# Transposing attention weights on VectorE and moving the blocks by DMA, in place of TensorE's transposes

## The chip, the cores and the metric

The kernel runs on one core of a Trainium2 chip. The metric is the time of one execution on the device in microseconds (us); several runs are taken and their median is given. The profile is that of one further execution. Its engines are TensorE (PE for matrix products, PEld for its loads of weights), VectorE (DVE), ScalarE (ACT), GpSimd (POOL) and SyncE (SP), which issues the DMA transfers here.

## The reference, cut to what matters

Four batches of attention with eight heads, 768 tokens and 64 features per head, followed by a gated feed-forward layer. Attention is local and blockwise at once: each token sees the tokens less than 16 away and, beside them, 24 summaries of blocks of 32 tokens (the maximum of the keys, the mean of the values).

```
k_sum = k.reshape(B, H, nb, block, D).max(axis=3)
v_sum = v.reshape(B, H, nb, block, D).mean(axis=3)
scores_l = where(|i - j| < 16, scale * q @ k.T, -1e9)
scores_s = scale * q @ k_sum.T + log(block)
a = softmax(concat(scores_l, scores_s))
x = a @ concat(v, v_sum)
...
xk = mu_k * x + (1 - mu_k) * x_prev ; xr = mu_r * x + (1 - mu_r) * x_prev
k = relu(xk @ w_k) ; out = sigmoid(xr @ w_r) * ((k * k) @ w_v)
```

## The kernel before

The work is cut into 32 units and 8 halves. A unit is one batch, one pair of heads and one half of the sequence (384 tokens, six windows of 64 queries); `unit` (L437) writes it down. A window sees 96 nearby keys and 24 block summaries, 120 columns in all (NK). A half is one batch and 384 tokens of the feed-forward layer: three gate products (`gate_tile`, L555) and eight expert steps (`experts`, L585), each a first product (L601) and a second product (L628).

In a unit, PE forms the scores of both heads into two PSUM tiles `sc` (L458). DVE applies the mask and takes the row's extreme (L469), ACT takes the exponential and its sum (L473), DVE inverts the sums (L479 and L480) and POOL scales the rows (L485). The weights then stand in the tiles `y` with queries on the partitions. The product with the values needs the keys on the partitions, so PE transposes three 128x120 blocks per head into a PSUM tile `pt` (L492), ACT copies them to SBUF as `pts` (L496), and PE multiplies by the values (L505). The result is copied into `vx` (L516 or L518), from which ACT, POOL and DVE make the inputs of the feed-forward layer (L527, L530, L533, L542, L544).

The transposes, the copies and the values product, cut from `unit`:

```
for i in range(NSL):
    nc.tensor.transpose(out=pt[h].t[0:NK, i * P:(i + 1) * P], in_=y[h].t[:, i, :], identity=ident_sb)
...
op("ACT", "pts", None, lambda h=h: nc.scalar.copy(
    out=pts[h].t, in_=pt[h].t[0:NK, 0:NSL * P].rearrange("p (i c) -> p i c", c=P)),
```

Loads of keys, values and queries (L359, L363, L441) go through SP. From batch 1 on the block means of the values come from a feature-major copy, loaded at L408, summed on DVE (L409), transposed on PE (L412), scaled on ACT (L429), and then spread by SP into six windows of each value tile (L432), SBUF to SBUF, two transfers per pair of heads. The feed-forward weights are loaded as words into the three staging tiles `st` (L323) and put together by ACT and DVE (L324, L327, L329); `split` (L333) makes a high and a low part of each, so that a full-precision product is three products of reduced-precision parts. In the first half of all, the first PLAIN expert steps (three here) skip the splitting and run as one plain fp32 product instead.

The order of all instructions is written out ahead by a planner (`Plan.schedule`, L143). Each operation has a cost from a table (LENGTH), the tiles it reads and writes, and a due time; each engine takes the operation that can start first, and among those ready the one that is due first. Operations inherit their due times from what follows them. The plan fixes the order of each engine's queue, SP's included; at run time semaphores decide when a step starts, and an engine never changes the order. The gate of half n is due at GATE1 + PERIOD x (n - 1), the first at GATE0; the units of a batch are due before its gate, UNITS apart from one another; the scores of a unit are due 10 us before the unit. SP takes a transfer at the earliest 20 us (EARLY) before it is due, keeps at most eight in flight (LANES) and costs 450 ns per issue (ISSUE) in the plan. Tiles come from pools of fixed size, most of them in the order in which the program asks for them: four `y`, three `pts` (one per head), three `st`, one `pt`, two `sc`, twelve `vx`.

Of the kernel before, what the change touches and what calls it, by code (L numbers as in the profile page):

```python
# [9 lines left out]
F32 = mybir.dt.float32  # L10
F32R = mybir.dt.float32r
U32 = mybir.dt.uint32
# [8 lines left out]
P = 128  # L21
NPAIR = H // 2
NS = S // BLOCK
QW = 64
# [17 lines left out]
    warm=223, kred=865, kred2=470, kmax=90, kcopy=280, vred=865, mask=204, rc=320, evac=470, mixd=535, sub=475, khv=280,  # L42
    result=600, wbits=340, wor=610, wsub=605, tiny=60,
    exp=380, pts=375, vm=160, mixa=515, cast=405, relu=380, square=425, sigmoid=500, sigmoid3=1600, wscale=570, wcast=530,
    norm=345, wcast_p=640, mixa_p=600, kcopy_p=450, evac_a=375,
)
TAIL = dict(PE=0, DVE=85, ACT=95, POOL=0, SP=0)
LATENCY = dict(PE=260, DVE=110, ACT=110, POOL=150, SP=0)
# [1 line left out]
DMA_FIXED = 2000  # L50
GATE0 = 34000
FULL = 34000
STEP0 = 4000
PLAIN = 3, 3
GATE1 = 76000
PERIOD = 50000
STEP = 4600
SLACK = 400
WARM = 260
WARM_END = 110000  # L60
GAP = 300
COLD = 5000
EARLY = 20000
ISSUE = 450
LANES = 8
TABLE = 1300
TABLES = dict(sigmoid=1, sigmoid3=1, exp=0, wscale=0)
LOCKS = {"wbits", "wor", "wsub", "mixd", "sub", "kcopy", "khv", "spread"}
FIRST = 4000
SECOND = 58000, 64000, 70000, 76000  # L70
UNITS = 5500


class Slot:
# [31 lines left out]
class Plan:  # L106
# [36 lines left out]
    def schedule(self):  # L143
# [29 lines left out]
        while any(ready.values()):  # L173
            best = None
            for e, now in engines.items():
                pick = fill = None
                if e == "PE" and now > WARM_END:
                    ready[e] = [x for x in ready[e] if x[0].name != "warm"]
                for o, at in ready[e]:
                    if o.name == "wcast" and len(free_slots["w"]) < owed + 2:  # L180
                        continue
                    if o.name == "warm":
                        fill = max(now, at), o
                        continue
                    start, need, ok = max(at, now, o.due - EARLY if e == "SP" else 0), {}, True
                    if e == "SP":
                        start = max(start, lanes[-LANES])
                    for x in o.bufs:
                        if x.place is None:
                            k = need.get(x.pool, 0)  # L190
                            if x.n not in (None, turn[x.pool] + k) or len(free_slots[x.pool]) <= k:
                                ok = False
                                break
                            start = max(start, free_slots[x.pool][k][0])
                            need[x.pool] = k + 1
                    if not ok:
                        continue
                    if any(max(start, engines[f]) + c < start + o.ways[e][0] for f, (c, _) in o.ways.items() if f != e):
                        continue
                    if e == "POOL" and o.name != "tiny" or e == "DVE" and o.name in LOCKS:  # L200
                        start = max(start, port)
                    late = start > now
                    load = e == "ACT" and TABLES.get(o.name, table) != table
                    key = (start if late else now, o.due + TABLE * load, o.n)
                    if pick is None or key < pick[0]:
                        pick = key, o, start
                if fill and (pick is None or pick[2] > fill[0] + GAP):
                    pick = None, fill[1], fill[0]
                if pick and (best is None or pick[2] < best[2]):
                    best = pick + (e,)  # L210
            assert best, "no operation can go on"
            _, o, start, e = best
            o.eng = e
            o.cost, o.emit = o.ways[e]
            owed += dict(wor=-1, wcast=1, wsub=-1).get(o.name, 0)
            for f in o.ways:
                ready[f] = [x for x in ready[f] if x[0] is not o]
            for x in o.bufs:
                if x.place is None:
                    _, x.place = free_slots[x.pool].pop(0)  # L220
                    turn[x.pool] += x.n is not None
            if e == "PE" and start < COLD:
                o.cost *= 1.6
            if e == "ACT" and TABLES.get(o.name, table) != table:
                o.cost += TABLE
                table = 1 - table
            o.start = start
            if e == "SP":
                engines[e] = start + ISSUE
                dma = max(dma, start + 600) + o.size * DMA_NS_PER_BYTE  # L230
                o.finish = dma + DMA_FIXED - 600
                lanes.append(o.finish)
            else:
                engines[e] = start + o.cost
                if e == "POOL" and o.name != "tiny" or e == "DVE" and o.name in LOCKS:
                    port = start + o.cost
                o.finish = start + o.cost + TAIL[e]
            for x in o.bufs:
                x.left -= 1
                if not x.left:  # L240
                    end = max(u.finish + LATENCY[u.eng] for u in x.users)
                    pool, places = self.later.get(x.pool, (x.pool, [x.place]))
                    free_slots[pool].extend((end, place) for place in places)
                    free_slots[pool].sort(key=lambda s: s[0])
            order.append(o)
            for s in o.succ:
                waiting[s] -= 1
                if not waiting[s]:
                    released(s)
# [4 lines left out]
def tile_kernel(ctx: ExitStack, tc: tile.TileContext, q, k, vT, v, mask, ident, pool, sel, mu, w_k, w_v, w_r, out):  # L254
# [7 lines left out]
    def slots(name, n, shape):  # L262
# [5 lines left out]
        ktx=[last_kt], w=slots("w", 2 * (NCK + 2 * NCV), [P, 512]),  # L268
        kt=tiles("kt", 3, [P, KL]), qt=tiles("qt", 4, [P, HT]), vx=tiles("vx", 12, [P, S + 1]),
        kg=tiles("kg", 2, [P, 49]), ks=tiles("ks", 2, [P, NS]),  # L270
        vs=tiles("vs", 1, [P, NS]), vm=tiles("vm", 4, [P, P]), sp=tiles("sp", 2, [P, P]),
        y=tiles("y", 4, [P, NSL, NK]), mn=tiles("mn", 4, [P, NSL]), sm=tiles("sm", 3, [P, 2 * NSL]),
        rc=tiles("rc", 3, [P, 2 * NSL]), pts=tiles("pts", 3, [NK, NSL, P]),
        z=tiles("z", 4, [P, DM]), xa=tiles("xa", 4, [P, HT]),
        xs=slots("xs", 16, [P, HT]), r=tiles("r", 2, [P, HT]),
        kh=tiles("kh", 2, [P, HT], F32R), kl=tiles("kl", 2, [P, HT], F32R),
# [76 lines left out]
    def load_set(b, p):  # L353
# [74 lines left out]
        else:  # L428
            op("ACT", "vm", None, lambda: nc.scalar.activation(  # L429
                vm.t[0:NS], tp.t[0:NS, 0:P], AF.Copy, scale=1.0 / BLOCK), reads=[(tp, 0)], writes=[(vm, 0)])  # L430
            for x in vw:
                op("SP", "load", None, lambda x=x: nc.sync.dma_start(  # L432
                    out=windows(x)[QW:KB], in_=vm.t[0:NS].unsqueeze(1).broadcast_to([NS, HW, P])),
                   reads=[(vm, 0)], writes=[(x, "b")], size=NS * HW * 512)
        return e

    def unit(b, p, hf, e, due):  # L437
# [6 lines left out]
        y = [buf("y") for _ in range(2)]  # L444
        mn = [buf("mn") for _ in range(2)]
        sm, rc = buf("sm"), buf("rc")
        pt = [buf("pt") for _ in range(2)]
        pts = [buf("pts") for _ in range(2)]
        av = buf("av")


        def scores():
# [7 lines left out]
                            start=True, stop=True,  # L460
                        )

        op("PE", "score", due - 10000, scores, reads=[*e["kparts"], (kt, "s"), (qt, 0)],
           writes=[(sc[0], 0), (sc[1], 0)])
        for h in range(2):
            for i in range(NSL):
                slot = hf * NSL + i
                var = 0 if slot == 0 else (2 if slot == 2 * NSL - 1 else 1)
                op("DVE", "mask", None, lambda h=h, i=i, var=var: nc.vector.tensor_tensor_reduce(  # L469
                    out=y[h].t[:, i, :], in0=sc[h].t[:, i, 0:NK], in1=mask_sb[:, var, :], scale=-SCALE, scalar=3.0e38,  # L470
                    op0=ALU.add, op1=ALU.min, accum_out=mn[h].t[:, i:i + 1]),
                   reads=[(sc[h], 0), *MASK], writes=[(y[h], i), (mn[h], i)])
                op("ACT", "exp", None, lambda h=h, i=i: nc.scalar.activation(  # L473
                    y[h].t[:, i, :], y[h].t[:, i, :], AF.Exp, bias=mn[h].t[:, i:i + 1], scale=-1.0,
                    accum_out=sm.t[:, NSL * h + i:NSL * h + i + 1]),
                   reads=[(y[h], i), (mn[h], i)], writes=[(y[h], i), (sm, NSL * h + i)])

# [5 lines left out]
        for h in range(2):  # L483
            for i in range(NSL):
                op("POOL", "norm", None, lambda h=h, i=i: nc.gpsimd.tensor_scalar(  # L485
                    out=y[h].t[:, i, :], in0=y[h].t[:, i, :], scalar1=rc.t[:, NSL * h + i:NSL * h + i + 1],
                    scalar2=1.0, op0=ALU.mult, op1=ALU.mult),
                   reads=[(y[h], i), (rc, 0)], writes=[(y[h], i)])

            def transposes(h=h):  # L490
                for i in range(NSL):
                    nc.tensor.transpose(out=pt[h].t[0:NK, i * P:(i + 1) * P], in_=y[h].t[:, i, :], identity=ident_sb)  # L492

            op("PE", "transpose", due - 3500 + 800 * h, transposes,
               reads=[(y[h], i) for i in range(NSL)] + [*IDENT], writes=[(pt[h], 0)])
            op("ACT", "pts", None, lambda h=h: nc.scalar.copy(  # L496
                out=pts[h].t, in_=pt[h].t[0:NK, 0:NSL * P].rearrange("p (i c) -> p i c", c=P)),
               reads=[(pt[h], 0)], writes=[(pts[h], 0)])

        def values():  # L500
            for w in range(HW):
                i, c = divmod(w, 2)
                for h in range(2):
                    hs = slice(h * D, (h + 1) * D)
                    nc.tensor.matmul(  # L505
                        av.t[hs, w * QW:(w + 1) * QW], windows(vw)[:, w, hs], pts[h].t[:, i, c * QW:(c + 1) * QW],
                        start=True, stop=True,
                    )

        op("PE", "values", due - 1000, values, reads=[(vw, x) for x in "ab"] + [(pts[0], 0), (pts[1], 0)],  # L510
           writes=[(av, 0)])
        if hf == 0:
            xt = xts[b, p] = buf("vx")
# [163 lines left out]
        weight("wv", j, w_v[j], j == NCV - 1)  # L677

    op("POOL", "tiny", -1.0e6, lambda: nc.gpsimd.memset(zero_sb, 0.0), writes=ZERO)
    spare = pools["pt"][0][:, 512 - P:512]  # L680
    for _ in range(WARM):
        op("PE", "warm", 1.0e8, lambda: nc.tensor.matmul(spare, zero_sb, zero_sb, start=True, stop=True), reads=ZERO)
# [123 lines left out]
```

## Time and profile before

| what | value |
|---|---|
| median of 3 runs | 449.93 us (449.85 to 450.32) |
| the profiled execution's own time | 450.6 us |
| its span, from the first to the last instruction | 448.8 us |
| granted clock of TensorE, mean over the span | 1.00 |
| transposes of the attention weights (L492) | 192 instructions |
| values products (L505) | 768 instructions, 24 a unit |
| transfers that spread the block means (L432) | 24 |

A line of the stretches view gives the busy time of each engine between two points of the span. A line of the chain gives when a piece began, how long it lasted and whose it was; the chain is followed back from the last instruction, at each step to what released it. An engine listed with q, as SPq or PEldq, is that engine's own queue of instructions. The profiled execution's own time is 1.8 us above its span, and 0.7 us above the median.

### The profile page before, as it was taken

To read this page: it belongs to the slowest core of one execution; us is meant where nothing else is said; L and a number is where in the kernel's file an instruction comes from. 1 tells how busy PE (TensorE), PEld (TensorE's weight loads), DVE (VectorE), ACT (ScalarE), POOL (GpSimd) and SP (SyncE) were. 2 spreads that over 40 slices of the span, in tenths; PEclk is the share of its full clock that TensorE was granted. 3 is DMA by queue.
4 is the path that set the end of the run, shared out by engine and by line. 5 is a ranking of instruction groups with operands and counts; after the bars stand their busy time and mean duration, and the time that the engine had idled before them with its cause. 6 is when DMAs were issued, how large, how long until landed. Compare 5 with 4: busy or idle time off the path is not lost.

```text
span 448.8 us, 9629 instructions
## 1 busy us (share of the span) xinstructions
PE 441.7 (98%) x3521; PEld 366.3 (82%) x3521; DVE 261.2 (58%) x866; ACT 282.9 (63%) x808; POOL 104.8 (23%) x237
## 2 busy tenths in 40 slices
PE   8999999999999999999999999999999999999996
PEld 8755578778888888978888888987888888888895
DVE  3889998995645763194655756175663455232213
ACT  3798999997765583288866655268966555232221
POOL 0561545561540012032432012002442001000000
PEclk9999999999999999999999999999999999999999
DMA  8967886831024275051007076031000010001001
GB/s 288 395 225 253 318 300 225 273 136 39 15 71 150 77 246 200 2 169 31 15 2 272 2 243 229 0 125 64 15 15 15 1 71 1 1 0 72 0 0 72
DMA packets 24230, 51.96 MB, mean 116 GB/s; under 512 B 2935, under 2 KB 10743, under 8 KB 24183
## 3 DMA queue, kind: packets, MB, share of 16 engines
q1 hardware_dynamic: 24183, 51.35, 33.3%
q8 instruction: 28, 0.46, 0.4%
q14 instruction: 19, 0.16, 0.1%
HBM read 43.28 MB, written 6.29 MB: 110 GB/s over the span
## 4 chain that ended last, share of the span: by engine, by line
PE 90%; ACT 3%; DMA 3%; DVE 2%; SPq 1%; issue 0%; DVEq 0%
PE mm L628 30%; PE mm L601 29%; PE av L505 5%; PE pt L492 5%; PE sc L458 4%; PE mm L562 4%; PE mm L564 4%; PE mm L563 4%; DMA vx<-in_v 3%; PE mm L575 2%; ACT y L473 1%; PE pt L412 0%; DVE z L658 0%; ACT pts L496 0%; PE mm L397 0%
## 5 line engine op out<-in xcount | busy, mean ns | idle before, releaser
L601 PE MATMUL mm<-xs,w 128*128 128x384 f32 x756 | 147.4, 343 | 0.0
L601 PEld LDWEIGHTS mm<-xs,w 128*128 128x128 f32 x756 | 132.9, 188 | 7.4 <-issue 0.7
L485 POOL TENSOR_SCALAR y<-y,rc 128x120 f32<-128x120 f32 x192 | 83.9, 455 | 142.1 <-DVE rc L480 117.1
L628 PE MATMUL mm<-w,kh 128*128 128x512 f32 x366 | 100.3, 402 | 0.2 <-ACT kh L615 0.2
L608 ACT ACTIVATE r<-mm 128x384 f32<-128x384 f32 x64 | 31.3, 489 | 95.7 <-PE mm L601 95.7
L473 ACT ACTIVATE y<-y,mn 128x120 f32<-128x120 f32 x192 | 73.7, 387 | 13.2 <-DVE mn L469 13.1
L628 PEld LDWEIGHTS mm<-w,kh 128*128 128x128 f32 x366 | 66.1, 188 | 12.6 <-ACT kh L615 0.5
L614 DVE CAST kh<-r 128x384 fp32r<-128x384 f32 x55 | 21.1, 384 | 92.6 <-ACT r L610 83.6
L628 PE MATMUL mm<-w,kl 128*128 128x512 f32 x183 | 57.0, 406 | 0.0
L469 DVE CUSTOM_DVE_ANT_0 y<-sc,mask_sb 128x120 f32<-128x120 f32 x192 | 42.5, 276 | 16.1 <-PE sc L458 16.0
L544 DVE TENSOR_TENSOR xs<-xa,xs 128x384 fp32r<-128x384 f32 x56 | 30.5, 551 | 32.8 <-ACT xs L542 32.6
L628 PEld LDWEIGHTS mm<-w,kl 128*128 128x128 f32 x183 | 32.9, 188 | 7.4 <-issue 0.5
L533 DVE SCALAR_TENSOR_TENSOR xa<-vx,mu_sb,xa 128x384 f32<-128x384 f32 x56 | 33.5, 627 | 8.2 <-POOL xa L530 4.2
L616 DVE TENSOR_TENSOR kl<-r,kh 128x384 fp32r<-128x384 f32 x61 | 34.7, 569 | 4.2 <-ACT kh L615 0.7
L473 ACT ACTIVATION_READ_ACCUMULATOR y<-y,mn 128x1 f32 x192 | 36.4, 189 | 0.0
L610 ACT ACTIVATE r<-r 128x384 f32<-128x384 f32 x64 | 33.7, 526 | 1.2
L505 PEld LDWEIGHTS av<-pts,vx 120*64 120x64 f32 x768 | 25.1, 137 | 10.2 <-issue 6.4
L562 PE MATMUL mm<-w,xs 128*128 128x512 f32 x84 | 33.3, 397 | 0.0
L492 PE MATMUL pt<-ident_sb,y 128*120 128x128 f32 x192 | 32.5, 278 | 0.8 <-ACT pts L496 0.6
L496 ACT COPY pts<-pt 120x384 f32<-120x384 f32 x64 | 30.1, 470 | 5.0 <-PE pt L492 4.3
L564 PE MATMUL mm<-w,xs 128*128 128x512 f32 x84 | 32.9, 392 | 0.0
L563 PE MATMUL mm<-w,xs 128*128 128x512 f32 x84 | 32.8, 390 | 0.0
(65 smaller groups left out, 505.1 us busy)
## 6 DMA issues: line engine op xcount, KB each, us to landing
vx<-in_v SPq DMA_DIRECT2D x32, 384.0 KB
kt<-in_k SPq DMA_DIRECT2D x15, 544.0 KB
qt<-in_q SPq DMA_DIRECT2D x32, 192.0 KB
out<-z SPq DMA_DIRECT2D x24, 256.0 KB
st<-in_vT SPq DMA_DIRECT2D x12, 384.0 KB
st<-in_w_k SPq DMA_DIRECT2D x8, 512.0 KB
st<-in_w_v SPq DMA_DIRECT2D x8, 512.0 KB
st<-in_w_r SPq DMA_DIRECT2D x4, 512.0 KB
```

The costliest lines, as they stand in the source:

```text
L469: op("DVE", "mask", None, lambda h=h, i=i, var=var: nc.vector.tensor_tensor_reduce(out=y[h].t[:, i, :], in0=sc[h].t[:, i, 0:NK], in1=mask_ ...
L473: op("ACT", "exp", None, lambda h=h, i=i: nc.scalar.activation(y[h].t[:, i, :], y[h].t[:, i, :], AF.Exp, bias=mn[h].t[:, i:i + 1], scale=-1.0,
L485: op("POOL", "norm", None, lambda h=h, i=i: nc.gpsimd.tensor_scalar(out=y[h].t[:, i, :], in0=y[h].t[:, i, :], scalar1=rc.t[:, NSL * h + i: ...
L492: nc.tensor.transpose(out=pt[h].t[0:NK, i * P:(i + 1) * P], in_=y[h].t[:, i, :], identity=ident_sb)
L505: nc.tensor.matmul(av.t[hs, w * QW:(w + 1) * QW], windows(vw)[:, w, hs], pts[h].t[:, i, c * QW:(c + 1) * QW], start=True, stop=True,)
L562: nc.tensor.matmul(ps.t, xh.t[:, ts], h, start=(p == 0), stop=False)
L563: nc.tensor.matmul(ps.t, xh.t[:, ts], l, start=False, stop=False)
L564: nc.tensor.matmul(ps.t, xl.t[:, ts], h, start=False, stop=(p == NPAIR - 1))
L601: nc.tensor.matmul(ps.t[:, 0:HT], w.t[:, p * P:(p + 1) * P], x[p][s].t, start=(n == 0), stop=(n == len(terms) * NPAIR - 1))
L610: op("ACT", "square", None, lambda: nc.scalar.activation(r.t, r.t, AF.Square), reads=[(r, 0)], writes=[(r, 0)])
L616: op("DVE", "sub", None, lambda: nc.vector.tensor_tensor(out=kl.t, in0=r.t, in1=kh.t.bitcast(F32), op=ALU.subtract), reads=[(r, 0), (kh, 0 ...
L628: nc.tensor.matmul(acc[t].t, a.t[:, t * P:(t + 1) * P], v.bitcast(F32) if single else v, start=start, stop=stop)
```

## The change

For batches 1 to 3 PE's transposes and ACT's copies are taken out. DVE transposes each head's weights in 32x32 blocks (`flip`) into a staging tile of the pool `st`, laid out so that every partition holds four runs of 768 bytes. Sixteen transfers a unit (`move`), each of 32 partitions (24 where the last rows are padding) and one run per partition, carry the blocks to their partitions in `pts`. The tile `pts` now holds both heads and has a new inner order, [4, 2, NSL, 32], so that a values product reads its moving rows as two runs of 32 elements. Batch 0 keeps PE's transposes, with ACT's copy writing the new order.

Around that, `y` gets 128 columns per window, of which POOL zeroes the last eight once at the start; the pools `pts` and `vm` get one tile fewer; the scores of batches 1 to 3 are due 22 us (AHEAD) before their unit; PLAIN goes from 3 to 6 expert steps; the due times (STEP0, GATE1, PERIOD, STEP, UNITS) and the planner's issue costs change.

```diff
-STEP0 = 4000
-PLAIN = 3, 3
-GATE1 = 76000
-PERIOD = 50000
-STEP = 4600
+STEP0 = 6200
+PLAIN = 6, 6
+GATE1 = 92000
+PERIOD = 49000
+STEP = 4800
...
+AHEAD = 22000
...
+ISSUES = dict(move=380, spread=820)
...
-UNITS = 5500
+UNITS = 10500
...
-                    start, need, ok = max(at, now, o.due - EARLY if e == "SP" else 0), {}, True
+                    start, need, ok = max(at, now, o.due - EARLY if e == "SP" and o.name != "move" else 0), {}, True
...
-        y=tiles("y", 4, [P, NSL, NK]), mn=tiles("mn", 4, [P, NSL]), sm=tiles("sm", 3, [P, 2 * NSL]),
-        rc=tiles("rc", 3, [P, 2 * NSL]), pts=tiles("pts", 3, [NK, NSL, P]),
+        y=tiles("y", 4, [P, NSL, P]), mn=tiles("mn", 4, [P, NSL]), sm=tiles("sm", 3, [P, 2 * NSL]),
+        rc=tiles("rc", 3, [P, 2 * NSL]), pts=tiles("pts", 2, [P, 4, 2, NSL, 32]),
...
-        op("PE", "score", due - 10000, scores, reads=[*e["kparts"], (kt, "s"), (qt, 0)],
+        op("PE", "score", due - (10000 if b == 0 else AHEAD), scores, reads=[*e["kparts"], (kt, "s"), (qt, 0)],
...
+            if b > 0:
+                continue
             op("PE", "transpose", due - 3500 + 800 * h, transposes,
...
-                out=pts[h].t, in_=pt[h].t[0:NK, 0:NSL * P].rearrange("p (i c) -> p i c", c=P)),
-               reads=[(pt[h], 0)], writes=[(pts[h], 0)])
+                out=pts.t[0:NK, :, h].rearrange("p a i q -> p i a q"),
+                in_=pt[h].t[0:NK, 0:NSL * P].rearrange("p (i a q) -> p i a q", i=NSL, a=4)),
+               reads=[(pt[h], 0)], writes=[(pts, h)])
+        spots = [(pts, h) for h in range(2)]
+        if b > 0:
+            yt = buf("st", U32, False)
+
+            def turned():
+                return yt.t[:, 0:2 * NSL * P].bitcast(F32).rearrange("p (r h i q) -> p r h i q", r=4, h=2, i=NSL)
+
+            for h in range(2):
+                op("DVE", "flip", due - AHEAD + 8000 + 600 * h, lambda h=h: nc.vector.transpose(
+                    out=turned()[:, :, h], in_=y[h].t.rearrange("p i (r c) -> p r i c", r=4)),
+                   reads=[(y[h], i) for i in range(NSL)], writes=[(yt, h)])
+            spots = [(pts, f"m{c}{r}") for c in (2, 3, 0, 1) for r in range(4)]
+            for n, spot in enumerate(spots):
+                c, r = int(spot[1][1]), int(spot[1][2])
+                rows = min(32, NK - 32 * r)
+                op("SP", "move", due - 4500 - ISSUES["move"] * (len(spots) - 1 - n), lambda c=c, r=r, rows=rows: nc.sync.dma_start(
+                    out=pts.t[32 * r:32 * r + rows, c], in_=turned()[32 * c:32 * c + rows, r]),
+                   reads=[(yt, 0), (yt, 1)], writes=[spot], size=rows * 2 * NSL * 128)
...
-                        av.t[hs, w * QW:(w + 1) * QW], windows(vw)[:, w, hs], pts[h].t[:, i, c * QW:(c + 1) * QW],
+                        av.t[hs, w * QW:(w + 1) * QW], windows(vw)[:, w, hs], pts.t[0:NK, 2 * c:2 * c + 2, h, i],
...
-        op("PE", "values", due - 1000, values, reads=[(vw, x) for x in "ab"] + [(pts[0], 0), (pts[1], 0)],
+        op("PE", "values", due - 1000, values, reads=[(vw, x) for x in "ab"] + spots,
...
+    for t in pools["y"]:
+        op("POOL", "tiny", None, lambda t=t: nc.gpsimd.memset(t[:, :, NK:P], 0.0))
```

More of the change, by code (lines that the diff above doesn't have):

```diff
@@ L44 @@
     exp=380, pts=375, vm=160, mixa=515, cast=405, relu=380, square=425, sigmoid=500, sigmoid3=1600, wscale=570, wcast=530,
-    norm=345, wcast_p=640, mixa_p=600, kcopy_p=450, evac_a=375,
+    norm=345, wcast_p=640, mixa_p=600, kcopy_p=450, evac_a=375, flip=560,
 )
@@ L228, in schedule @@
             if e == "SP":
-                engines[e] = start + ISSUE
+                engines[e] = start + ISSUES.get(o.name, ISSUE)
                 dma = max(dma, start + 600) + o.size * DMA_NS_PER_BYTE
@@ L270, in tile_kernel @@
         kg=tiles("kg", 2, [P, 49]), ks=tiles("ks", 2, [P, NS]),
-        vs=tiles("vs", 1, [P, NS]), vm=tiles("vm", 4, [P, P]), sp=tiles("sp", 2, [P, P]),
-        y=tiles("y", 4, [P, NSL, NK]), mn=tiles("mn", 4, [P, NSL]), sm=tiles("sm", 3, [P, 2 * NSL]),
-        rc=tiles("rc", 3, [P, 2 * NSL]), pts=tiles("pts", 3, [NK, NSL, P]),
+        vs=tiles("vs", 1, [P, NS]), vm=tiles("vm", 3, [P, P]), sp=tiles("sp", 2, [P, P]),
+        y=tiles("y", 4, [P, NSL, P]), mn=tiles("mn", 4, [P, NSL]), sm=tiles("sm", 3, [P, 2 * NSL]),
+        rc=tiles("rc", 3, [P, 2 * NSL]), pts=tiles("pts", 2, [P, 4, 2, NSL, 32]),
         z=tiles("z", 4, [P, DM]), xa=tiles("xa", 4, [P, HT]),
@@ L431, in load_set @@
             for x in vw:
-                op("SP", "load", None, lambda x=x: nc.sync.dma_start(
+                op("SP", "spread", None, lambda x=x: nc.sync.dma_start(
                     out=windows(x)[QW:KB], in_=vm.t[0:NS].unsqueeze(1).broadcast_to([NS, HW, P])),
@@ L446, in unit @@
         sm, rc = buf("sm"), buf("rc")
-        pt = [buf("pt") for _ in range(2)]
-        pts = [buf("pts") for _ in range(2)]
+        pts = buf("pts")
+        pt = [buf("pt") for _ in range(2)] if b == 0 else None
         av = buf("av")
@@ L469, in unit @@
                 op("DVE", "mask", None, lambda h=h, i=i, var=var: nc.vector.tensor_tensor_reduce(
-                    out=y[h].t[:, i, :], in0=sc[h].t[:, i, 0:NK], in1=mask_sb[:, var, :], scale=-SCALE, scalar=3.0e38,
+                    out=y[h].t[:, i, 0:NK], in0=sc[h].t[:, i, 0:NK], in1=mask_sb[:, var, :], scale=-SCALE, scalar=3.0e38,
                     op0=ALU.add, op1=ALU.min, accum_out=mn[h].t[:, i:i + 1]),
@@ L473, in unit @@
                 op("ACT", "exp", None, lambda h=h, i=i: nc.scalar.activation(
-                    y[h].t[:, i, :], y[h].t[:, i, :], AF.Exp, bias=mn[h].t[:, i:i + 1], scale=-1.0,
+                    y[h].t[:, i, 0:NK], y[h].t[:, i, 0:NK], AF.Exp, bias=mn[h].t[:, i:i + 1], scale=-1.0,
                     accum_out=sm.t[:, NSL * h + i:NSL * h + i + 1]),
@@ L485, in unit @@
                 op("POOL", "norm", None, lambda h=h, i=i: nc.gpsimd.tensor_scalar(
-                    out=y[h].t[:, i, :], in0=y[h].t[:, i, :], scalar1=rc.t[:, NSL * h + i:NSL * h + i + 1],
+                    out=y[h].t[:, i, 0:NK], in0=y[h].t[:, i, 0:NK], scalar1=rc.t[:, NSL * h + i:NSL * h + i + 1],
                     scalar2=1.0, op0=ALU.mult, op1=ALU.mult),
@@ L491, in transposes @@
                 for i in range(NSL):
-                    nc.tensor.transpose(out=pt[h].t[0:NK, i * P:(i + 1) * P], in_=y[h].t[:, i, :], identity=ident_sb)
+                    nc.tensor.transpose(out=pt[h].t[0:NK, i * P:(i + 1) * P], in_=y[h].t[:, i, 0:NK], identity=ident_sb)
+            if b > 0:
+                continue
             op("PE", "transpose", due - 3500 + 800 * h, transposes,
```

## The prediction

> **What bounds the kernel now.** I read the busy shares of the page first, then the chain that ended last, then busy time by stretch, and then the pieces of the chain. A change of 0.2% (0.9 us) is about what a measurement of this kernel can tell from none.
>
> ```profile
> PE 441.7 (98%) x3521; PEld 366.3 (82%) x3521; DVE 261.2 (58%) x866; ACT 282.9 (63%) x808; POOL 104.8 (23%) x237
> PE 90%; ACT 3%; DMA 3%; DVE 2%; SPq 1%; issue 0%; DVEq 0%
> ```
>
> Every engine but PE has room on average, and 90% of the chain is PE. The stretches say where that holds (columns: stretch, length, then busy time of PE, PEld, DVE, ACT, POOL, granted clock, DMA share, GB/s).
>
> ```profile
> 17.00:40.00 23.00, 22.28 (x265) 13.67 (x256) 20.88 (x53) 19.91 (x57) 9.90 (x18) 1.00 0.74 267
> 40.00:62.00 22.00, 22.00 (x117) 12.41 (x117) 21.82 (x77) 21.94 (x60) 10.84 (x16) 1.00 0.87 303
> 62.00:85.00 23.00, 22.13 (x269) 18.35 (x271) 21.61 (x77) 22.02 (x75) 10.86 (x21) 1.00 0.74 260
> 105.00:160.00 55.00, 55.00 (x480) 46.79 (x479) 31.75 (x106) 35.87 (x105) 11.69 (x28) 1.00 0.26 81
> 310.00:370.00 60.00, 60.00 (x524) 50.97 (x524) 31.13 (x113) 41.50 (x121) 13.87 (x33) 1.00 0.09 25
> ```
>
> From 40 us on PE idles 0.9 us in 62 to 85 and not at all in the stretches of batches 1 and later shown here. There PE's work is the time: what leaves PE shortens the kernel one for one, until another engine or a transfer becomes later. Until 85 us three engines are full at once, so there a gain on PE is less certain.
>
> **What leaves PE.** The change takes six transposes out of each of the 24 units of batches 1 to 3: 144 of 192. Their price on the path comes from the chain between 105 and 160 us and the transposes counted in that stretch.
>
> ```profile
> by line: PE mm L628 31.9%; PE mm L601 30.8%; PE av L505 9.3%; PE pt L492 7.1%; PE sc L458 5.6%; PE mm L564 5.0%; PE mm L563 5.0%; PE mm L562 5.0%; PE pt L412 0.8%
> 105.00:160.00 55.00, 5.49 (x33) 4.03 (x33) 1.00 0.26 81
> ```
>
> 7.1% of 55 us is 3.9 us over 33 transposes, 0.118 us each; 144 of them make 17.0 us. The upper end is 17.0. Not all of that comes back, as the pieces of the chain show (start, length, piece).
>
> ```profile
> 110.00 0.85 PE av L505 x24
> 110.85 0.47 PE pt L492 x3
> 111.32 1.39 PE mm L628 x6
> 112.71 0.33 PE pt L492 x3
> 100.78 0.69 PE mm L628 x3
> 120.72 0.85 PE av L505 x24
> 121.57 0.89 PE mm L628 x3
> ```
>
> Three transposes cost 0.33 us, but 0.47 right behind the values product (av). A wide product behind av pays such a switch too: 0.89 against 0.69. So each group gives back 0.33, and the 0.14 behind av turns into up to 0.20. With 48 groups that is 15.8 us, less 24 x 0.06 = 1.4 if all groups that stood there pass the switch on: 14.4 at the lower end. I take 15.5, near the 15.8 of the common row.
>
> The Trainium skill ("VectorE: DVE Perf Modes", section Rules for kernel authors) speaks against this change: for a 128x128 transpose it says to use TensorE where a PSUM destination will do, and in its section The three transpose paths gives TensorE 390 ns and VectorE's 32x32 blocks 311 ns (bf16). By the 390 ns alone, 144 transposes would be worth 56 us, an estimate; the chain's 0.118 us each disagrees and decides.
>
> **What is added to PE.** PLAIN goes from 3 to 6: three more expert steps of the first half run as one plain product instead of three split ones.
>
> ```profile
> 50.44 2.58 PE mm L601 x8
> 53.02 2.58 PE mm L628 x6
> 63.23 2.10 PE mm L601 x12
> 65.33 2.10 PE mm L628 x9
> ```
>
> Each step is 2 x (2.58 - 2.10) = 0.96 us longer, 2.9 us for three. In return VectorE loses their casts and subtractions, and six weight splits are needed later; the most that can give is the 0.9 us that PE idles in 62 to 85. I count nothing for it.
>
> **The other engines.** ACT loses 48 copies (L496) and VectorE gains 48 flips of 128x384. No transpose of VectorE is in the trace; these are the nearest rows.
>
> ```profile
> L496 ACT COPY pts<-pt 120x384 f32<-120x384 f32 x64 | 30.1, 470 | 5.0 <-PE pt L492 4.3 <-PE pt L682 0.7
> L614 DVE CAST kh<-r 128x384 fp32r<-128x384 f32 x55 | 21.1, 384 | 92.6 <-ACT r L610 83.6 <-PE pt L492 9.0
> L516 DVE COPY vx<-av 128x384 f32<-128x384 f32 x12 | 6.7, 555 | 8.1 <-PE av L505 8.1
> ```
>
> A flip lies between 0.38 and 0.56 us; I take the dearer row, 0.56, as the careful end; the choice moves the sum only if VectorE binds. That is 1.1 us a unit on VectorE, which is idle 23 of 55 us in 105 to 160 (55 - 31.75): 7 units' worth there is 8 us, hidden. ACT's 0.94 us saved per unit is off the path as well. The four memsets of y's padding columns cost at most a norm each, 0.4 us (2.49 over six in the row of L485 further down), on POOL, idle for over half of each stretch above: nothing.
>
> **The transfers.** Each unit issues 16 moves on SP, in front of or behind loads, spreads and stores on the same queue.
>
> ```profile
> 131.93 0.36 SPq L441 DMA_DIRECT2D qt<-in_q  x1
> 132.34 0.43 SPq L408 DMA_DIRECT2D st<-in_vT  x1
> 133.29 0.43 SPq L363 DMA_DIRECT2D vx<-in_v  x1
> L432 SPq DMA_DIRECT2D vx<-vm x24: 778/786/949, 83.3 to 339.9; - x24
> 339.00:346.00 7.00, 7.00 (x52) 6.24 (x52) 2.32 (x14) 4.35 (x18) 3.02 (x7) 1.00 0.12 23
> 116.27 14.98 SPq L432 DMA_DIRECT2D vx<-vm  x4
> 220.96 14.98 SPq L432 DMA_DIRECT2D vx<-vm  x4
> 0.74 0.39 SPq L359
> 3.36 0.55 DVE L373 TENSOR_REDUCE kg<-kt 128x24 f32<-128x384 f32 x1 [3.36 <-DMA kt<-in_k]
> ```
>
> A load with one run per row has SP for 0.36 to 0.43 us, a start every 0.45 us on average (131.93 to 133.29 is three starts); a spread, with six runs per row, 0.79, some 0.83 with the gap. A move has one run per row, as a load, so I take 0.38 to 0.45, and 0.83 as the far end. A unit costs SP 6.1 to 7.2 us in moves, plus its share of the rest: a batch has 24 loads, 8 spreads and 6 stores, 24 x 0.45 + 8 x 0.83 + 6 x 0.45 = 20.1 us, 2.5 a unit. Together 8.6 to 9.7. A batch now lasts 104.7 us (the same stores of rows at 116.27 and 220.96), after the change 104.7 - 15.5/3 = 99.5, or 12.4 a unit: SP would be 70 to 78% full and hold. As for the engines that carry the bytes: the two spreads in 339 to 346 are 288 packets of 512 bytes at 12% of 16 engines, 47 ns a packet; a unit's 16 x 30.5 = 488 packets of 768 bytes at 47 to 70 ns are 1.4 to 2.1 us of all sixteen, hidden in 12.4.
>
> From issue to use, the first load (280 KB) takes 3.36 - 0.74 = 2.6 us; a move of 24 KB takes less than that. Flip to last landed byte is then at most 7.2 + 2.6 = 9.8 us. Before it stand scores, softmax and norm.
>
> ```profile
> 119.94 0.78 PE sc L458 x24
> 123.98 0.17 DVE L479 TENSOR_SCALAR sm<-sm 128x6 f32<-128x6 f32 x1
> 117.98 2.49 POOL L485 TENSOR_SCALAR y<-y,rc 128x120 f32<-128x120 f32 x6 [2.12 <-DVE rc L480]
> ```
>
> Scores to sums 4.2 us, inverse 0.4, norm 2.5, flips 1.1, moves 9.8: 18 us. The plan asks for scores at 22 us and values at 1 us before the unit's due time, 21 us apart: it fits by 3. If flips come late by more than that, moves stand at the head of SP and hold loads and stores behind them, and values holds all of PE.
>
> Values now waits for many transfers, for up to eight semaphores if the moves rotate over the plan's eight lanes (LANES). One extra wait is a 51 ns instruction on PE's loader queue.
>
> ```profile
> L505 PEldq EVENT_SEMAPHORE  x3: 51/51/51, 333.1 to 348.2; - x3
> 335.92 0.92 PE L505 MATMUL av<-pts,vx 120*64 120x64 f32 x24
> ```
>
> Eight are 0.41 us a unit, 9.8 us over 24 units if bare. But the wait at 333.1 was passed 2.8 us before its product began at 335.92: the queue runs ahead, and the 0.41 us lies under products already queued. I take 0.05 us a unit, 1.2 in all. The price of losing that cover is the 9.8. The values product reads its moving rows in two runs of 32, which no row here shows: nothing at the low end; at double price 32 x 0.85 = 27 us; I take nothing, by the row of the same product with the same number of elements, 0.85.
>
> **Sum.** -15.5 + 2.9 + 1.2 = -11.4 us, on the profiled execution's 450.6 us (span 448.8 and 1.8 around it): 439.2. The median of the runs, 449.93, is 0.7 lower, so 438.5. Bounds: 17.0 - 2.9 + 0.9 = 15.0 of gain, 434.9; with 14.4, 2.9 and the full 9.8 of waits a gain of 1.7, 448.2.
>
> **Rivals.**
>
> First, the ramp of batch 1. Its eight units need 69 to 78 us of SP (8 x 8.6 to 9.7).
>
> ```profile
> 82.04 0.28 PE L412 MATMUL pt<-ident_sb,vs 128*24 128x128 f32 x1
> 149.45 0.23 PE mm L562
> 69.86 0.33 SPq L323 DMA_DIRECT2D st<-in_w_v  x1
> ```
>
> Now they run between the first pooled values at 82 and the gate of batch 1 at 149: 67 us. If the new plan starts them no earlier, PE waits 2 to 11 us there once: 440 to 449. For it: the buffers (the flips land in the weights' three staging tiles, and weights load until 69.86) and the full engines until 85. Against it: the first unit is now due at 92 + 49 - 14 - 73.5 = 53.5 us instead of 73.5, and removed copies and splits leave room. Chance 0.15.
>
> Second, slower: SP's queue becomes the bound in all of batches 1 to 3. To lose more than 0.9 us on 449.93, 12.3 us must be eaten, 4.1 a batch: 103.6 / 8 = 12.95 us a unit, less 2.5 is 10.45, or 0.65 us a move. From there on SP sets the pace; at the spread's 0.83 a unit takes 15.8 us, a batch 126, three batches 80 us more: 518. For it: the spread's row is also an SBUF-to-SBUF transfer. Against it: the six runs per row, which a move lacks. Chance 0.12, the doubled read of values (466) included. The Trainium skill ("DMA: Bandwidth & Descriptors", Rules for kernel authors) says the same side: coalesce small transfers, under 64 KB one pays mostly overhead; with its fixed 2.0 us each, one after the other, 16 moves would be 32 us, an estimate. The spreads' landing under PE's work here, with no idle of PE put down to them, speaks against such a series.
>
> Third, no change: all that leaves PE comes back as bare waits (9.8) and a little ramp (1.6). 450. Chance 0.04.
>
> The forecast's own case has 0.69, at 435 to 444: from the lower bound to half of the waits bare (438.5 + 4.9). The range reaches to 449, over the ramp, and leaves out the last two rivals (0.16) and little below 434.5. Faster: 0.69 + 0.15 = 0.84; same 0.04; slower 0.12.
>
> **What would show it.** Right: L492 down to 48 transposes; the chain without them in 105 to 350; PE without idle there; the batch period near 99.5; a move at 0.33 to 0.45 us of SP; a flip at 0.4 to 0.56. Wrong: idle of PE before the values products put down to DMA; SP starts over 0.6 us apart; av over 0.85 us a unit; a gate of batch 1 later than 152.

## The result, and the profile after

The changed kernel takes 534.17 us in the median (531.43 to 536.67, 4 runs), the kernel before 450.12 (449.85 to 450.88, 4 runs): a ratio of 1.186 (95% interval 1.180 to 1.193). The forecast was 438.5 with a range to 449. It was wrong in sign, and by far. The profiled execution took 534.97 us, its span is 533.2.

First the page of the changed kernel: busy shares, and the chain that ended last by engine and by line (L519 issues the moves, L651 and L624 are the expert products).

```profile
PE 459.9 (86%) x3376; PEld 375.7 (70%) x3376; DVE 277.9 (52%) x900; ACT 270.3 (51%) x763; POOL 113.4 (21%) x248
PE 36%; SPq 30%; DMA 12%; ACT 10%; DVE 7%; issue 4%; POOL 0%; DVEq 0%; ACTq 0%; POOLq 0%
SPq L519 26%; PE mm L651 13%; PE mm L624 11%; DMA kt<-in_k 3%; DMA vx<-vm 2%; DMA vx<-in_v 2%; ACT y L475 2%; PE mm L585 2%; PE mm L587 2%; PE mm L586 2%; PE av L528 2%; DMA pts<-st 2%; PE sc L460 2%; SPq L434 2%; ACT wc L326 2%
```

Before, PE had 90% of the chain and SP's queue 1%. Now SP's queue has 30%, and 26% of the whole span is the issuing of moves. The stretches (stretch, length, busy time of PE, PEld, DVE, ACT, POOL, granted clock, DMA share, GB/s) show from where on:

```profile
62.00:85.00 23.00, 23.00 (x206) 13.97 (x205) 22.33 (x85) 22.90 (x73) 12.80 (x23) 1.00 0.66 221
105.00:160.00 55.00, 36.63 (x274) 30.71 (x274) 19.29 (x60) 20.56 (x52) 7.41 (x18) 0.82 0.22 61
310.00:370.00 60.00, 49.74 (x377) 41.01 (x377) 32.42 (x119) 30.98 (x98) 13.87 (x30) 0.91 0.32 105
460.00:500.00 40.00, 40.00 (x198) 35.67 (x197) 10.71 (x22) 10.44 (x21) 0.00 (x0) 1.00 0.05 20
```

Until 85 us PE is as full as before. From 105 to 160 PE is busy 36.6 of 55 us where it was busy all 55, and the other engines' busy time falls with it: all of them wait. The DMA engines that carry the bytes are not what is full; they are busy 22% there. The granted clock, 1.00 before, is 0.82 there, and it is back at 1.00 where PE is full again. The timeline of PE says what ended its idle time (in brackets, before each values product):

```profile
119.71 1.55 PE L528 MATMUL av<-pts,vx 120*64 120x64 f32 x24 [6.59 <-DMA pts<-st]
131.33 1.55 PE L528 MATMUL av<-pts,vx 120*64 120x64 f32 x24 [3.25 <-DMA pts<-st]
143.79 1.40 PE L528 MATMUL av<-pts,vx 120*64 120x64 f32 x24 [4.54 <-DMA pts<-st]
```

They come 12 us apart, each behind the landing of a move. Over the whole span (total us, times, longest) as much of this idle ends with a spread of the block means, which stands behind moves on the same queue:

```profile
PE av L528 <- DMA vx<-vm: 28.7, 8, 6.4
PE av L528 <- DMA pts<-st: 26.2, 7, 6.6
```

And this is SP's own timeline over the same time (start, length, and the number of transfers merged into the row), with the group of all moves below it (shortest, median and longest time that one holds SP, in ns):

```profile
81.11 10.71 SPq L519 DMA_DIRECT2D pts<-st  x16
91.92 1.70 SPq L434 DMA_DIRECT2D vx<-vm  x2
94.31 22.41 SPq L519 DMA_DIRECT2D pts<-st  x32
117.80 10.58 SPq L519 DMA_DIRECT2D pts<-st  x16
129.39 11.51 SPq L519 DMA_DIRECT2D pts<-st  x16
```
```profile
L519 SPq DMA_DIRECT2D pts<-st x384: 507/589/1559, 81.1 to 426.4; - x192
```

In the median a move holds SP for 0.589 us, and with the gap behind it starts stand 0.66 to 0.72 us apart (10.58 / 16 to 11.51 / 16). From 81 to 428 us SP's timeline shows three pauses over 0.7 us, of 1.6, 10.3 and 1.4 us. 347 us for 24 units are 14.5 us a unit. That is the kernel's pace. What the change was to do, it did:

```profile
L512 DVE STREAM_TRANSPOSE st<-y 128x384 f32<-128x384 f32 x48 | 26.9, 568 | 26.3 <-DMA vx<-vm 9.3
L494 PE MATMUL pt<-ident_sb,y 128*120 128x128 f32 x48 | 8.3, 281 | 0.0
```

48 transposes are left on PE, and a flip takes 0.568 us on DVE.

### The profile page after: what moved, and what is told of

The parts are those of the page before. It is cut to its first block, busy times and chain, and to the rows that moved or that the text cites. A ratio compares the mean times of both kernels' runs of the same rounds, so it can differ in the third digit from the quotient of the medians.

```text
span 533.2 us, 9806 instructions
## 1 busy us (share of the span) xinstructions
PE 459.9 (86%) x3376; PEld 375.7 (70%) x3376; DVE 277.9 (52%) x900; ACT 270.3 (51%) x763; POOL 113.4 (21%) x248
## 4 chain that ended last, share of the span: by engine, by line
PE 36%; SPq 30%; DMA 12%; ACT 10%; DVE 7%; issue 4%; POOL 0%; DVEq 0%; ACTq 0%; POOLq 0%
SPq L519 26%; PE mm L651 13%; PE mm L624 11%; DMA kt<-in_k 3%; DMA vx<-vm 2%; DMA vx<-in_v 2%; ACT y L475 2%; PE mm L585 2%; PE mm L587 2%; PE mm L586 2%; PE av L528 2%; DMA pts<-st 2%; PE sc L460 2%; SPq L434 2%; ACT wc L326 2%
## 5 line engine op out<-in xcount | busy, mean ns | idle before, releaser
L624 PE MATMUL mm<-xs,w 128*128 128x384 f32 x744 | 157.5, 362 | 0.0
L624 PEld LDWEIGHTS mm<-xs,w 128*128 128x128 f32 x744 | 139.0, 199 | 12.3 <-issue 2.3
L487 POOL TENSOR_SCALAR y<-y,rc 128x120 f32<-128x120 f32 x192 | 86.4, 468 | 244.5 <-DVE rc L482 228.6
L651 PE MATMUL mm<-w,kh 128*128 128x512 f32 x348 | 98.8, 414 | 0.2 <-ACT kh L638 0.2
L528 PE MATMUL av<-pts,vx 120*64 120x64 f32 x768 | 37.2, 260 | 64.3 <-DMA vx<-vm 28.7
L528 PEld LDWEIGHTS av<-pts,vx 120*64 120x64 f32 x768 | 32.6, 169 | 76.3 <-issue 54.2
L651 PEld LDWEIGHTS mm<-w,kh 128*128 128x128 f32 x348 | 66.8, 197 | 13.3 <-issue 0.9
L637 DVE CAST kh<-r 128x384 fp32r<-128x384 f32 x48 | 17.3, 360 | 89.3 <-ACT r L633 89.2
L651 PE MATMUL mm<-w,kl 128*128 128x512 f32 x174 | 57.6, 427 | 0.2 <-DVE kl L639 0.2
L541 ACT COPY vx<-av 128x384 f32<-128x384 f32 x25 | 12.0, 481 | 59.7 <-PE av L528 59.7
L651 PEld LDWEIGHTS mm<-w,kl 128*128 128x128 f32 x174 | 34.1, 202 | 9.2 <-DVE kl L639 0.7
L512 DVE STREAM_TRANSPOSE st<-y 128x384 f32<-128x384 f32 x48 | 26.9, 568 | 26.3 <-DMA vx<-vm 9.3
L460 PE MATMUL sc<-kt,qt 64*64 64x120 f32 x768 | 32.2, 301 | 3.1 <-DMA qt<-in_q 2.7
L585 PE MATMUL mm<-w,xs 128*128 128x512 f32 x84 | 33.8, 402 | 0.0
```

The source lines that it names most:

```text
L460: nc.tensor.matmul(sc[h].t[cs, i, 0:NK], qt.t[hs, n * QW:(n + 1) * QW], kt.t[hs, w * KB:w * KB + NK], start=True, stop=True,)
L528: nc.tensor.matmul(av.t[hs, w * QW:(w + 1) * QW], windows(vw)[:, w, hs], pts.t[0:NK, 2 * c:2 * c + 2, h, i], start=True, stop=True,)
L585: nc.tensor.matmul(ps.t, xh.t[:, ts], h, start=(p == 0), stop=False)
L624: nc.tensor.matmul(ps.t[:, 0:HT], w.t[:, p * P:(p + 1) * P], x[p][s].t, start=(n == 0), stop=(n == len(terms) * NPAIR - 1))
L651: nc.tensor.matmul(acc[t].t, a.t[:, t * P:(t + 1) * P], v.bitcast(F32) if single else v, start=start, stop=stop)
```

## The experiments

Theory Q: SP's queue is the bound, since a move by its nature holds SP for about 0.6 us. Its rivals: W (waits and traffic stretch a cheap issue), D (the moved bytes, their landing, the eight waits or the split rows of the values product), P (the plan's order, made with the wrong cost), C (the new due times and the plain steps).

**What an issue costs by itself.** A kernel of its own, without the computation: it stores zeros and issues groups of small transfers, one group a line.

> This kernel leaves the whole computation out: it stores zeros and issues groups of 16 small transfers of 768-byte rows (8 of 1536-byte rows in one group), each group from one line, so that SP's time per transfer can be read by group: HBM to SBUF with 128, 32 and 24 rows; SBUF to SBUF with 128, 24, 16 and 32 rows; then the 32-row form issued by ACT, by POOL, and by SP and ACT together. Theory Q (a move by its nature holds SP for about 0.6 us, start to start 0.67): the SBUF-to-SBUF groups show 0.6 to 0.7 us start to start without any other work beside them, and the loads 0.4 to 0.5. Rival W (the move is a cheap issue, stretched in the changed kernel by waits for its lane and by traffic): 0.38 to 0.48 in all groups.

Its timeline of SP (16 transfers a row, 14 in the first, 8 in L46's), then of ACT's queue, then the group that POOL issued (x16 | busy us, mean ns):

```profile
17.73 7.04 SPq L31 DMA_DIRECT2D la<-in_q  x14
24.81 7.38 SPq L33 DMA_DIRECT2D lb<-in_q  x16
32.24 6.50 SPq L35 DMA_DIRECT2D lc<-in_q  x16
38.87 10.50 SPq L37 DMA_DIRECT2D ma<-yt  x16
49.41 12.28 SPq L40 DMA_DIRECT2D mc<-yt  x16
61.73 10.06 SPq L43 DMA_DIRECT2D md<-yt  x16
71.84 5.03 SPq L46 DMA_DIRECT2D mh<-yt  x8
76.92 10.09 SPq L49 DMA_DIRECT2D mb<-yt  x16
```
```profile
86.41 10.16 ACTq L52 DMA_DIRECT2D lw<-mb  x16
```
```profile
L55 POOL DMA_DIRECT2D mq<-lw x16 | 8.0, 505 | 94.9 <-DMA lw<-mb 94.9
```

From HBM, 128, 32 and 24 rows: 0.50, 0.46 and 0.41 us each. From SBUF to SBUF, 128, 24, 16 and 32 rows: 0.66, 0.77, 0.63 and 0.63. Twice the bytes per row (L46): 0.63 again. So here the price hangs on where the data comes from and goes to, and hardly on how much it is; 24 rows cost more than 32 (0.77 is above what was expected), and every fourth move has 24. The time that one issue itself holds SP shows the same (shortest, median, longest, in ns): 32 rows from HBM, then 24 and 32 rows from SBUF to SBUF.

```profile
L33 SPq DMA_DIRECT2D lb<-in_q x16: 419/420/428, 24.8 to 31.8; - x16
L40 SPq DMA_DIRECT2D mc<-yt x16: 713/714/852, 49.4 to 61.0; - x16
L49 SPq DMA_DIRECT2D mb<-yt x16: 588/589/590, 76.9 to 86.4; - x16
```

Three moves of 0.63 and one of 0.77 make 0.67 each, with nothing beside them; in the kernel it was 0.66 to 0.72. W is out, but for a few hundredths. ACT pays the same, POOL 0.50; SP and ACT issuing at once slowed each other little (10.07 and 10.42 us for 16 each).

**Four transfers in place of sixteen.**

```diff
-            spots = [(pts, f"m{c}{r}") for c in (2, 3, 0, 1) for r in range(4)]
+            spots = [(pts, f"m{c}") for c in (2, 3, 0, 1)]
...
-                    out=pts.t[32 * r:32 * r + rows, c], in_=turned()[32 * c:32 * c + rows, r]),
+                    out=pts.t[0:NK, c], in_=turned()[0:NK, c]),
```

> The changed kernel with a unit's sixteen moves replaced by four of 120 rows and 768 bytes each: the same bytes, but every block stays on the partitions where it is, so the attention weights reach the wrong keys and the output is not the reference's. All other work is the same. Theory Q (SP's issues set the pace): SP needs 4 x 0.5 + 3 = 5 us a unit instead of 14.4 and has room; the time falls to the forecast's 438 +- 5 us and the granted clock returns to 1.00. Rival D (the bytes' way, the waits of the values products on eight semaphores or their split moving rows cost the time): stays over 490 us. Rival P (the order of the plan is what is wrong): in between.

445.77 us, ratio 0.989 (0.984 to 0.993), clock 0.99: 1.1% faster than before, 88 us under the change, with the same bytes moved. Of D the bytes fall; the values products wait for fewer semaphores and landings here, and that part is left to the run with two queues below. A move of 120 rows holds SP 0.80 us, more than the 0.5 that I expected, but four make 3.2 us a unit. But 445.8 is not within 438 +- 5, and the stretches show where the rest lies; behind them, pieces of the chain.

```profile
85.00:105.00 20.00, 15.84 (x203) 11.75 (x202) 14.71 (x70) 13.79 (x56) 11.14 (x30) 0.91 0.56 159
205.00:265.00 60.00, 60.00 (x444) 50.64 (x443) 40.01 (x126) 40.91 (x108) 15.29 (x35) 1.00 0.44 144
```
```profile
98.46 2.43 DMA vx<-vm
...
221.52 0.85 PE av L527 x24
222.37 0.78 PE sc L460 x24
223.14 2.30 PE mm L623 x12
```

Later PE is full again, and the values product takes its 0.85 us: the split rows cost nothing. Between 85 and 105 us PE idles 4.2 us, for the units of batch 1. The spread in the chain takes 2.4 us from its release to its landing, its issue included.

**The plan told the true cost.**

```diff
-ISSUES = dict(move=380, spread=820)
+ISSUES = dict(move=680, spread=900)
```

> The changed kernel with the planner told what a move and a spread were measured to cost SP: 680 and 900 ns in ISSUES in place of 380 and 820. The computation is whole. Theory Q: SP still needs 14 us a unit, 24 units from 81 us on end at 420 or so and the rest of the feed-forward layer follows: 500 to 520 us. Rival P (a plan made with the wrong cost puts moves, loads and stores in an order in which PE waits needlessly): under 470 us.

506.66 us, ratio 1.124 (1.118 to 1.130). A plan that knows the costs gets back 27 of the 84 us; the rest is the queue.

```profile
L519 SPq DMA_DIRECT2D pts<-st x384: 507/589/1890, 81.7 to 419.4; - x192
```

The last move still starts at 419, and the last values product at 424.1 us in place of 430.1. Most of what the plan gains lies behind that: from there to the end of the span are 80 us in place of 103, with 396 matrix products left for PE in place of 492, so more of the feed-forward layer was done while the queue issued. P is a third of the loss, not its cause.

**The change without its moves.** TensorE's transposes and the copies of `pts` back in all batches, all else as in the change.

```diff
-            if b > 0:
-                continue
...
-        if b > 0:
+        if b > B:
             yt = buf("st", U32, False)
```

> The changed kernel with TensorE's transposes and ACT's copies back in all batches, no flips and no moves, but with the new due times, PLAIN of 6, scores due 22 us ahead and one pts tile for both heads. The computation is whole. Theory Q: no move, so no queue: 449.9 + 2.9 for the three plain steps, 453 us, within 4. Rival C (the new due times or the plain steps are what costs the time): over 470 us.

454.71 us, ratio 1.009 (1.006 to 1.012). C falls.

**Five larger transfers, by way of HBM.**

```diff
+            op("SP", "move", due - 9000, lambda: nc.sync.dma_start(out=hop.t, in_=yt.t[:, 0:2 * NSL * P].bitcast(F32)),
...
+                    in_=hop.t[:, r * 2 * NSL * 32:(r + 1) * 2 * NSL * 32].rearrange("(c p) e -> p c e", c=4)),
```

> The changed kernel with a unit's sixteen moves replaced by five larger transfers with the same result: one store of the flipped tile to a scratch tile in HBM (128 rows of 3072 bytes) and four loads from it, one per 32 keys (32 rows of four runs of 768 bytes). Computation whole, due times and PLAIN as in the change, the planner told 500 ns an issue. Theory Q: SP holds about 0.4 to 0.5 us for each of these, 2.5 us a unit in place of 11.2, and is no bound; 440 to 447 us, like the run with four transfers, with no idle of PE after 110 us. Rival D (the way of the bytes, landing late): the way through HBM takes two landings one after the other, 5 us a unit, so later than sixteen moves, and the time stays over 470.

445.58 us, ratio 0.989 (0.986 to 0.991): the whole computation, and the four-transfer kernel's time. The store holds SP 0.35 us, a load 0.42, with four runs a row. The stretches on both sides of the first gate of batch 1:

```profile
L517 SPq DMA_DIRECT2D hop<-st x24: 326/346/2097, 82.4 to 332.3; - x24
L521 SPq DMA_DIRECT2D pts<-hop x96: 303/424/1326, 87.4 to 336.2; - x96
```
```profile
85.00:105.00 20.00, 17.12 (x236) 12.65 (x234) 16.85 (x78) 16.18 (x64) 13.50 (x34) 1.00 0.68 196
105.00:160.00 55.00, 52.65 (x424) 45.11 (x417) 34.99 (x112) 36.88 (x98) 10.77 (x28) 1.00 0.60 191
```

PE idles 2.9 and 2.4 us there. I expected none after 110 us; that was missed.

**The moves dealt out to two queues.**

```diff
+                way = n % QUEUES
...
+                   lambda c=c, r=r, way=way: (nc.sync, nc.gpsimd)[way].dma_start(
+                    out=pts.t[32 * r:32 * r + 32, c], in_=turned()[32 * c:32 * c + 32, r]),
```

> The changed kernel with the sixteen moves dealt out in turn to SP and to POOL, eight each, all with 32 rows; the planner told 640 ns on SP and 500 on POOL. Computation whole. Theory Q (one queue's issue time): SP needs 8 x 0.63 + 3 = 8 us a unit and POOL 8 x 0.5 + 2.8 = 6.8, both under the 10.6 us that the plan gives a unit; 440 to 450 us. Rival D (sixteen small transfers a unit are the cost wherever issued: lanes, semaphores, landing): over 480.

446.87 us in the median of ten runs (443.24 to 452.27), ratio 0.991 (0.988 to 0.994). Sixteen small transfers a unit are no harm if SP issues eight and POOL eight: eight held SP 5.4 us, and the 192 of POOL 0.507 each. With that the rest of D falls too.

```profile
126.17 5.39 SPq L523 DMA_DIRECT2D pts<-st  x8
```
```profile
L523 POOL DMA_DIRECT2D pts<-st x192 | 96.1, 507 | 32.5 <-issue 16.8 <-PE mm L655 8.1 <-PE mm L628 4.0
```

The Trainium skill ("DMA: Bandwidth & Descriptors", sections Rules for kernel authors and Issuing engines are not separate DMA queues) says that spreading DMAs over several issuing engines only saves the sequencer's issue time, usually small against the transfer. One issue is short here too, 0.63 us against the 2.4 us of a spread's landing. But issues stand in a row on their queue, and sixteen a unit were the bound, so sharing them (with 32 rows in every move, and the plan told the costs) was worth 87 us: what is small for one transfer was not small in sum.

**The cost without the change.** The kernel before, with sixteen idle transfers a unit added that nobody reads; the planner is told 380 ns for each, as in the change.

```diff
+        for n in range(16 if b else 0):
+            c, r = divmod(n, 4)
+            op("SP", "move", due - 4500 - 380 * (15 - n), lambda n=n, c=c, r=r: nc.sync.dma_start(
+                out=junk[32 * r:32 * r + 32, c % 2], in_=mask_sb.rearrange("p a k -> p (a k)")[32 * c:32 * c + 32, 0:192]),
...
```

> The kernel before the change, transposes on TensorE and all, with sixteen SBUF-to-SBUF transfers of 32 rows and 768 bytes added to SP's queue in each unit of batches 1 to 3; they copy a piece of the mask to a place that nobody reads. Computation whole. Theory Q (SP's time alone, nobody waiting for the moved bytes): SP needs 16 x 0.64 + 3 = 13 us a unit, 24 units from about 80 us end at 390 to 410, and the last two halves' 96 us follow: 480 to 520 us. Rival D (the wait for the landed bytes or the split rows cost the time): under 455.

551.14 us, ratio 1.224 (1.220 to 1.228): the added issues, with nothing waiting for their bytes, reproduce the loss and more. PE's wait is for the spreads that stand behind the idle transfers on SP's queue (total us, times, longest); the last line is SP's own wait:

```profile
L504 SPq DMA_DIRECT2D junk<-mask_sb x384: 507/589/1889, 73.0 to 445.8; - x192
```
```profile
PE av L513 <- DMA vx<-vm: 53.3, 14, 10.7
SPq L443 <- PE sc L460: 33.7, 5, 9.6
```

The size was missed by 31 us. Its SP stands still for six stretches of 6 to 10 us between 180 and 360, about 50 us in all, where the changed kernel's has one. In four of them a load of queries (L443) at the head of the queue waits for scores (L460), in two a store waits for results, so part of this loss is the order of the queue. The old due times, which bunch the units before their gates, would explain that, but I did not test it.

**Where the rest of the forecast's gain went.** The way through HBM for batches 2 and 3 alone, PLAIN 3, due times set anew:

```diff
-STEP0 = 6200
-PLAIN = 6, 6
-GATE1 = 92000
+STEP0 = 4000
+PLAIN = 3, 3
+GATE1 = 76000
...
-STEP = 4800
-UNITS = 10500
+STEP = 5000
+UNITS = 5500
...
-            if b > 0:
+            if b >= 2:
```

> The way through HBM for batches 2 and 3 only (16 units), TensorE's transposes for batches 0 and 1, PLAIN 3 as before the change, due times set anew. Computation whole. Theory Q with the ramp as the second cost: no plain steps (2.9 to 4 us less than in the change), no late batch 1, 16 x 0.64 = 10 us gained on PE: 437 to 443 us, faster than before by over 1.5%. If the ramp of batch 1 was not what kept the four-transfer kernel above 438, this one ends no better than that kernel, 445.

440.44 us, ratio 0.978 (0.976 to 0.980). Then from the third unit of batch 1 on (MOVED = 10, with PERIOD 47000 and AHEAD 16000), its control with TensorE's transposes in all units (MOVED = 99, which also puts all scores 10 us before their units), and PLAIN 6 alone in the kernel before:

```diff
+MOVED = 10
...
-            if b > 0:
+            if 8 * b + 2 * p + hf >= MOVED:
```

> The way through HBM from the third unit of batch 1 on (22 units; the first two of batch 1 and all of batch 0 keep TensorE's transposes), PLAIN 3, due times set anew. Computation whole. Theory Q with the ramp as the second cost: 22 x 0.64 = 14 us off PE, no plain steps, and the first units of batch 1 no later than before: 434 to 439 us. If every unit of batch 1 that goes the long way delays its gate, no better than the run with batches 2 and 3 alone, 440.

> The control to the run before it: the same due times and PLAIN, but TensorE's transposes in all 32 units. Computation whole. If the gain of that run and of the one with batches 2 and 3 comes from the transposes taken off PE: the time of the kernel before, 450 +- 2. If it comes from the due times: under 445.

> The kernel before the change with PLAIN 6 in place of 3 and nothing else. Computation whole. The forecast's term: 3 x 0.96 = 2.9 us more on PE, so 453 +- 1 us. If fewer casts and splits on the full engines before 85 us help PE: 450 to 451.

438.71 us, ratio 0.975 (0.972 to 0.977), the best of all; the control 450.71, ratio 1.001 (0.999 to 1.004); PLAIN 6 alone 453.74, ratio 1.008 (1.005 to 1.011). The best version's page and stretches:

```profile
PE 428.5 (98%) x3393; PEld 354.1 (81%) x3393; DVE 277.5 (64%) x899; ACT 272.9 (63%) x776; POOL 106.5 (24%) x242
```
```profile
85.00:105.00 20.00, 19.65 (x195) 15.79 (x194) 19.54 (x72) 19.78 (x60) 11.52 (x27) 1.00 0.59 181
105.00:160.00 55.00, 54.37 (x422) 46.48 (x421) 36.75 (x107) 33.82 (x91) 10.55 (x25) 1.00 0.57 191
```

PE is full again but for 1.0 us in these two stretches, with 13 us less to do (441.7 - 428.5). The gain comes with the transposes off PE: the due times alone give nothing. Its first gate product of batch 1 starts at 147.1 us, against 149.3 before and 156.5 in the kernel that sends all of batch 1 through HBM.

## Why the prediction was wrong

**The step that failed** is the price of a move on SP: "A move has one run per row, as a load, so I take 0.38 to 0.45, and 0.83 as the far end." Two rows were at hand, a load with one run per row from HBM and a spread with six runs per row from SBUF to SBUF. I took the number of runs for what sets the price. The first experiment shows that it is the way: from HBM to SBUF 0.41 to 0.50, from SBUF to SBUF 0.63 to 0.77. The runs count for little: with the same 24 rows, six runs each cost some 0.83 and one run 0.77. Nor is the source alone what costs, for the stores of rows from SBUF to HBM hold SP only 0.34 us in the kernel before:

```profile
L662 SPq DMA_DIRECT2D out<-z x24: 332/340/470, 97.6 to 445.8; - x24
```

In the kernel a move's start to start was 0.66 to 0.72. The row that I set aside, 0.83, was the nearer one. All four signs of being wrong that the prediction names came; the gate of batch 1, for one, started at 191.7 us.

**The point from which it decides** was off as well. I gave SP a batch period over eight units, 12.4 us a unit after the change and 12.95 to break even, hence 0.65 us a move. But the last two halves run without units: 24 units fit into the time from the first pooled values at 82 us to the last values at 351.5, 270 us, 11.2 a unit. Less the 2.5 us of other issues, 8.7 / 16 = 0.54 us a move. At 0.70 a move my formula gave 13.7 us a unit, 110 a batch, 10 over the 99.5 of the forecast, and 469 us in all. (That formula rests on a batch period of 104.7 us, read from rows that are spreads, not stores; from gate to gate the trace gives the same, 253.97 - 149.29.) The second rival was right in kind and place and too small: 24 units at the trace's 14.5 us, begun at 81, end at 428, the last values product starts at 430.1, and 103 us follow to the end (97 before). That is the result. About 27 us of it come from the plan that was made with the wrong cost, which no rival had. I gave the second rival 0.12.

**What the lost cover cost besides.** PE's clock was granted at 0.82 to 0.91 in the stretches between 85 and 370 us, where it idled. Many values products took 1.55 us in place of 0.92, and the mean over the span was 0.93. The Trainium skill ("DMA: Bandwidth & Descriptors", Rules for kernel authors) was on the right side with its advice to coalesce; the fixed cost per transfer, 2.0 us in the page's section Anatomy of one DMA (for transfers issued from GpSimd), was not what bound here: SP issued a move every 0.7 us, while a spread took 2.4 us to land, so transfers overlapped.

**Transposes off PE**, 15.5 us over 24 units or 0.65 a unit: right. Between the first gates of batches 1 and 3 the four-transfer kernel takes 197.6 us and the kernel with TensorE's transposes and the same due times 208.0: 10.4 us over 16 units, 0.65. The best version and its control differ by 12.0 us over 22 units, 0.55 a unit, somewhat less.

**The plain steps**, 2.9 us: 453.74 - 450.46 = 3.3, right; nothing came back from the lighter engines.

**A flip** at 0.38 to 0.56 us, taken 0.56: 0.568. **The split moving rows**, taken as nothing: 0.85 us as before, right. **The waits of the values products**: with sixteen moves on two queues PE idled 0.7 us in 205 to 310, so 1.2 us was not too little.

**The ramp of batch 1**, first rival, 2 to 11 us: with SP relieved, PE idled 2.9, 2.4 and 1.3 us in the three stretches from 85 to 205 us of the way through HBM, 6.5 in all. Right in place and size, but not by SP, which had room with five transfers a unit. In the best version, in which the first two units of batch 1 keep TensorE's transposes, PLAIN is 3 and the due times are others, 1.0 us is left in the first two of these stretches. Which of these edits removes it, and whether the longer way, the full engines before 85 us or the buffers make those units late, was not told apart.

## What to carry to other kernels

Price an issue by the row with the same source and destination, not by the one with the same shape: here that was 0.63 us against 0.45, sixteen times a unit. Add up every queue's issue time over the stretch in which the work must really fit, leaving out the stretches without such work, and ask where its break-even lies; a queue at 75% by an optimistic row is a queue that may bind. When a small-transfer step is off the compute engines, first cut the number of transfers or share them out among idle queues, and leave the first units of a ramp on the short way.

## What the runs showed of the hardware that was not expected

An issue from SBUF to SBUF held SP longer than one from HBM (0.59 against 0.42 us for 32 rows). The number of rows mattered and the bytes did not: 24 rows held SP longer than 32 (0.71 against 0.59), and 120 longer than 128 (0.80, in the kernel with four transfers, against 0.60); why was not tested. POOL issued the same transfer in 0.50 us, less than SP or ACT. The granted clock fell to 0.72 in a stretch where PE was busy two thirds of the time (the kernel with idle transfers, 275 to 310 us: 23.6 of 35, the line below); where PE was full it was 1.00.

```profile
275.00:310.00 35.00, 23.63 (x178) 19.96 (x178) 7.61 (x26) 11.68 (x33) 2.84 (x9) 0.72 0.18 43
```
